# Forgetting attention with a feed-forward layer on one core: the first twelve heads' exponentials go through TensorE transposes instead of an exchange through DRAM

## The chip, the cores and the metric

The kernel runs on one core of one Trainium2 chip. The metric is the device time of the core in microseconds, the median of the runs; smaller is better. Profiled times come from one execution and are counted from the start of its span.

## The reference

Eight batches of eight heads, 576 positions, 64 values per head. All is float32, and the products must come out at nearly that precision.

```python
scores = scale * np.matmul(q, k.transpose(0, 1, 3, 2))
decay = cum[:, :, :, None] - cum[:, :, None, :]      # cum: running sum of log f
scores = np.where(causal, -1e9, scores + decay)
attn = np.exp(scores - scores.max(-1, keepdims=True))
attn = attn / (attn.sum(-1, keepdims=True) + 1e-9)
x = np.matmul(attn, v)          # then tokens x 512
h = x @ w_in                    # 512 -> 2048
out = np.maximum(0.01 * h, h) @ w_out
```

## The kernel before

**Two kinds of work share TensorE.** One is attention, head by head. The other is the feed-forward layer over groups of 256 tokens, 18 of them, cut into pieces that the program calls quanta. A quantum is either half of a pair of hidden blocks (12 matmuls of 256 columns, tile `h`) or half of its product with `w_out` (6 matmuls of 512 columns, tile `o`). `fill(n)` (line 756) takes the next quanta of the generator `ffn` (line 671) and puts them between attention's steps. A float32 product is made of three matmuls on rounded high parts and low parts; that is why each operand is split, `gh` by VectorE and `gl` by GpSimd for the hidden values.

**An early stage** computes the first 256 tokens of three batches, with the order left to the framework's scheduler, which places each instruction where its own estimate finds its engine free. These heads' exponentials are transposed on TensorE (tile `tre`). Thirty-six quanta are placed in this stage.

**The main stage** then goes through 64 heads, here called head 0 to head 63 (`t` in the program). Heads 0 to 39 have all five chunks of query rows, 64 rows in the first and 128 in each of the others; heads 40 to 63 leave out the rows that the early stage has done. From line 810 on (`ordered[0] = True`) every engine keeps the order in which the program issues. That order comes from a table, `PLANS`: each head has eight slots, `scores` of chunk i stands in slot i, and every other step of head `t` stands a given number of slots after the head's first. One head goes so:

- `load` (278) fetches `qraw` and `kraw`; `load_decay` (440) fetches two rows of decays into the operands `s2` and `m2`; `prepare` (448) fills the rest of `s2` and `m2` by two ScalarE copies and two GpSimd subtractions; `split` (460) makes `s1` and `m1` by two ScalarE copies. `s1`, `m1`, `qraw` and `kraw` have one buffer each, `s2` and `m2` two (`a` for even heads, `b` for odd ones, which lets heads be told apart in the trace).
- `scores` (481) has two matmuls for each of six score tiles (`sc`, two buffers in PSUM; the last chunk has two tiles). VectorE subtracts the decay mask and takes the row maximum (out `z`, `max`), ScalarE takes the exponential in place.
- `turn` (530) transposes the exponentials in blocks of 32 by 32 on VectorE, from `z` to `zt`. `send` (555) writes `zt` to DRAM in four DMAs and `receive` (563) reads it back into `pl`, so that the blocks come to lie as the 128 by 128 transposes. This is done in two parts, chunks 0 to 2 and chunks 3 and 4. `divide` (569) rounds `pl` into the high part `ph` on ScalarE and leaves the low part in `pl` on VectorE.
- `values` (577) has 16 matmuls of `ph` and `pl` with the values (tile `av`, which shares two PSUM buffers, tag `tr`, with `rt`); `add` collects two heads in `x`. After each odd head, `inverse`, `spread_inverse` and `fetch_inverse` bring the inverse row sums through DRAM (`rt`, `inv`, `rb`), and `normalise` writes `x` to DRAM (`xd`), where the feed-forward layer fetches it. A batch's tokens are ready for the layer after its eighth head is normalised, 18 slots after that head's first, so in the second head behind it.

How many quanta go into a head is set when it begins: the quanta ready by then, divided by the heads until the batch after is ready and three more, at most nine. All of SyncE's DMAs stand in one queue in the program's order, each behind what the one ahead of it waits for.

Of the kernel before, what the change touches and what calls it, by code (L numbers as in the profile page):

```python
# [8 lines left out]
F32 = mybir.dt.float32  # L9
F32R = mybir.dt.float32r  # L10
# [4 lines left out]
ALU = mybir.AluOpType  # L15
# [61 lines left out]
def forgetting_attention_ffn(ctx, tc, qT, kT, v4, vr, f, w_in, w_out, out):  # L77
# [101 lines left out]
    def minus(out, a, b):  # L179
        nc.gpsimd.tensor_tensor(out, a, b, op=ALU.subtract)  # L180
# [91 lines left out]
    def places(t):  # L272
        return PLANS[0 if t < NEAR else 2 if tasks[t][1] else 1]

# [143 lines left out]
    def fix():  # L418

        for x in "ab":  # L420
            for w, n in (("s2", 2), ("m2", 4)):
                m = S + REST if w == "s2" else S
                y = fixed[w + x] = one.tile([P, m], F32R, tag=w + x, name=f"fixed_{w}{x}")
                nc.gpsimd.memset(y[:D].bitcast(F32), 0.0)
                nc.gpsimd.memset(y[:n].bitcast(F32), 1.0)
                if w == "s2":
                    nc.gpsimd.memset(y[:, :REST].bitcast(F32), 0.0)
            y = fixed["sum" + x] = one.tile([P, 2, NCH], F32, tag="sum" + x, name=f"fixed_sum{x}")
            nc.gpsimd.memset(y, 1.0)
        zt[0] = one.tile([P, 4 * FW], F32, tag="zt", name="zt")  # L430
        nc.gpsimd.memset(zt[0], 0.0)
        for w in ("ph", "pl"):
            fixed[w] = one.tile([P, 4 * FW], F32R, tag=w, name=f"fixed_{w}")
# [4 lines left out]
        nc.gpsimd.memset(vm[:, :, NFULL], 0.0)  # L438

    def load_decay(t):  # L440

# [6 lines left out]
    def prepare(t):  # L448

        s, c0, c1 = tasks[t]  # L450
        h = state[t]
        a, n = c0 * P, width(c1 - 1)
        x = "ab"[t % 2]
        s2, m2 = h["s2"], h["m2"] = fixed["s2" + x][:, REST:], fixed["m2" + x]
        for y, x, lo in ((s2, h["q"], a), (m2, h["k"], 0)):
            nc.scalar.copy(y[D:, lo:n], x[D:, lo:n])
        minus(h["q"][D:, a:n], h["q"][D:, a:n], s2[D:, a:n].bitcast(F32))
        minus(m2[D:, :n], h["k"][D:, :n], m2[D:, :n].bitcast(F32))

    def split(t, which=0):  # L460

# [19 lines left out]
    def scores(t, i):  # L481
# [2 lines left out]
        h = state[t]  # L484
        m, n, at = rows(t, i), width(i), width(i) - P
        part = slice(P - m, P)
        z = h[f"z{i}"] = one.tile([P, n], F32, tag="z" + "ab"[i % 2], name=f"z{i}_{t}")
        z = z[part]
# [16 lines left out]
        if i == NCH - 1 and t + 1 < len(tasks) and places(t)["SIN"]:  # L505
            split(t + 1)
        last = i + len(parts) - 1
        nc.scalar.activation(
# [15 lines left out]
    def unit(t, i, j):  # L524

        if tasks[t][1]:
            return 0, PW, (3 * j if j < 4 else 11) + i - 2 - max(j - 2, 0)
        return *(A if i < B[2] else B)[:2], FULL[i, j]

    def turn(t, i):  # L530
# [21 lines left out]
        base, w, u = unit(t, i, i)  # L552
        nc.vector.transpose(ap(zt[0][part], base + u * Q, [w, 2]), z[:, i * P:i * P + 2 * Q])

    def send(t, part):
# [21 lines left out]
    def values(t, part):  # L577
# [14 lines left out]
        for y, tile_ in enumerate(("ph", "pl")):  # L592
            for j in range(hi):
                i = max(j, lo)
                u = base + unit(t, i, j)[2] * Q
                a = fixed[tile_][:, u:u + 1]
                a = bass.AP(tensor=a.tensor, offset=a.offset, ap=[a.ap[0], [w, 4], [1, (hi - i) * Q]])
# [209 lines left out]
            values_of(x)  # L807
        fill(FQ[x])
    fix()
    beside[0] = ordered[0] = True  # L810
    load(0)
    load_decay(0)
    prepare(0)
    split(0)

    def spread(t, i):

        if tasks[t][1] and not tasks[t - 1][1] and i == 2:
            nc.gpsimd.memset(zt[0][:, :4 * PW], 0.0)
        turn(t, i)  # L820

    def finish(t):
        normalise(t)
# [13 lines left out]
    def load_next(t):  # L837
# [1 line left out]

    N, WT = 8, (1, 1, 1, 1, 1, 1, 1, 1)  # L840
    RANK = [
        split_next, receive, send, load_next, inverse, spread_inverse, divide, values, add, finish, prepare_next,
        load_decay_next, split_v, load_v, fetch_inverse,
    ]
    load(1)
    todo = {}
    for t in range(nt):
        part = int(not tasks[t][1])
        odd = tasks[t][0] % 2
        w = places(t)  # L850
# [22 lines left out]
    for at in range(N * nt + 3 * N):  # L873
# [52 lines left out]
```

## Time and profile before

| | us |
|---|---|
| median of three runs | 1207.67 (1207.54 to 1211.1) |
| the profiled execution's own time | 1206.35 |
| its span, first to last instruction | 1204.6 |
| TensorE busy | 1138.7 |
| VectorE, ScalarE, GpSimd busy | 746.9, 705.7, 445.6 |

Busy time of TensorE includes the overlapping ends of pipelined matmuls. The granted clock is the share of TensorE's full clock, 0.978 on the mean. "Idle before" a group of instructions is time in which its engine had nothing, and the name behind the arrow is what ended it.

### The profile page before, as it was taken

To read this page: it belongs to the slowest core of one execution; us is meant where nothing else is said; L and a number is where in the kernel's file an instruction comes from. 1 tells how busy PE (TensorE), PEld (TensorE's weight loads), DVE (VectorE), ACT (ScalarE), POOL (GpSimd) and SP (SyncE) were. 2 spreads that over 40 slices of the span, in tenths; PEclk is the share of its full clock that TensorE was granted. 3 is DMA by queue.
4 is the path that set the end of the run, shared out by engine and by line. 5 is a ranking of instruction groups with operands and counts; after the bars stand their busy time and mean duration, and the time that the engine had idled before them with its cause. 6 is when DMAs were issued, how large, how long until landed. Compare 5 with 4: busy or idle time off the path is not lost.

```text
span 1204.6 us, 21918 instructions
## 1 busy us (share of the span) xinstructions
PE 1138.7 (95%) x7148; PEld 1010.4 (84%) x7148; DVE 746.9 (62%) x1982; ACT 705.7 (59%) x1555; POOL 445.6 (37%) x353
## 2 busy tenths in 40 slices
PE   9999888879998999999999999999999998989998
PEld 6677777768897998889998899899989997778987
DVE  6878367776675767657676766655567666752221
ACT  7877466766666656666666665555565556541111
POOL 1001434434453445435454444453445454522000
PEclk9999899989998999989999999999999999999999
DMA  6654477876767776776766666656556566651000
GB/s 220 198 181 162 121 220 217 252 220 203 237 203 216 223 230 187 217 223 191 220 199 207 196 217 194 194 167 185 173 179 206 173 193 211 197 175 35 31 18 19
DMA packets 145714, 220.12 MB, mean 183 GB/s; under 512 B 21760, under 2 KB 104560, under 8 KB 145600
## 3 DMA queue, kind: packets, MB, share of 16 engines
q1 hardware_dynamic: 145600, 218.72, 59.7%
q8 instruction: 57, 0.93, 0.3%
q14 instruction: 57, 0.47, 0.1%
HBM read 141.87 MB, written 76.78 MB: 182 GB/s over the span
## 4 chain that ended last, share of the span: by engine, by line
PE 65%; ACT 9%; DVE 9%; DMA 9%; issue 5%; SPq 3%; POOL 1%; ACTq 0%; DVEq 0%; POOLq 0%
PE o L60 25%; PE h L60 24%; PE av L60 6%; PE sc L60 5%; DVE fixed_pl L60 3%; ACT z L60 3%; DMA fixed_pl<-zd 3%; SPq L60 3%; ACT fixed_ph L60 2%; DMA qraw<-in_qT 2%; DVE z L60 2%; PE ave L60 2%; DMA inv<-rt 1%; DMA zd<-zt 1%; PE sce L60 1%
## 5 line engine op out<-in xcount | busy, mean ns | idle before, releaser
L60 PE MATMUL h<-xh,win_h 128*128 128x256 f32 x1152 | 330.5, 287 | 0.4 <-ACT xh L60 0.4
L60 PE MATMUL h<-xh,win_l 128*128 128x256 f32 x1152 | 325.6, 283 | 0.0
L60 PE MATMUL h<-xs,win_h 128*128 128x256 f32 x1024 | 289.1, 282 | 0.0
L60 ACT ACTIVATE z<-z,max 64x64 f32<-64x64 f32 (+3 forms) x272 | 160.5, 590 | 211.8 <-DVE max L60 209.7
L60 POOL TENSOR_TENSOR gl<-g,gh 128x512 fp32r<-128x512 f32 x119 | 154.7, 1300 | 215.4 <-DVE gh L60 191.8
L60 PE MATMUL o<-wout_h,gh 128*128 128x512 f32 x576 | 234.4, 407 | 0.0
L60 PE MATMUL o<-wout_l,gh 128*128 128x512 f32 x576 | 230.0, 399 | 0.0
L60 PE MATMUL o<-wout_h,gl 128*128 128x512 f32 x576 | 229.6, 399 | 0.0
L60 PEld LDWEIGHTS h<-xh,win_h 128*128 128x128 f32 x1152 | 219.9, 191 | 5.7 <-ACT xh L60 0.9
L60 PEld LDWEIGHTS h<-xh,win_l 128*128 128x128 f32 x1152 | 220.0, 191 | 0.1
L60 DVE TENSOR_TENSOR fixed_pl<-fixed_pl,fixed_ph 128x768 fp32r<-128x768 f32 x168 | 158.7, 975 | 98.7 <-ACT fixed_ph L60 98.7
L60 DVE CUSTOM_DVE_ANT_0 z<-sc,tri 64x64 f32<-64x64 f32 (+3 forms) x272 | 123.7, 455 | 133.6 <-PE sc L60 127.1
L60 PEld LDWEIGHTS h<-xs,win_h 128*128 128x128 f32 x1024 | 195.5, 191 | 3.3
L60 DVE STREAM_TRANSPOSE zt<-z 64x64 f32<-64x64 f32 (+4 forms) x528 | 163.2, 346 | 40.8 <-ACT z L60 34.5
L60 ACT ACTIVATE g<-h 128x512 f32<-128x512 f32 x144 | 85.7, 595 | 155.4 <-PE h L60 139.7
L60 DVE CAST gh<-g 128x512 fp32r<-128x512 f32 x144 | 72.2, 501 | 115.4 <-ACT g L60 113.8
L60 ACT CAST fixed_ph<-fixed_pl 128x768 fp32r<-128x768 f32 x168 | 120.6, 755 | 28.5 <-DMA fixed_pl<-zd 27.4
L60 PE MATMUL sc<-m,fixed_s 128*128 128x64 f32 (+2 forms) x336 | 104.4, 316 | 30.0 <-DVE max L60 24.1
L60 PEld LDWEIGHTS o<-wout_h,gl 128*128 128x128 f32 x576 | 109.3, 190 | 26.3 <-POOL gl L60 0.7
L60 PEld LDWEIGHTS o<-wout_h,gh 128*128 128x128 f32 x576 | 109.9, 191 | 18.4 <-issue 0.5
L60 PEld LDWEIGHTS o<-wout_l,gh 128*128 128x128 f32 x576 | 110.0, 191 | 17.6 <-issue 0.3
L60 POOL TENSOR_TENSOR fixed_vs<-fixed_vm,fixed_vs 128x320 fp32r<-128x320 f32 x64 | 70.5, 1101 | 93.1 <-ACT fixed_vs L60 56.1
(116 smaller groups left out, 1669.1 us busy)
## 6 DMA issues: line engine op xcount, KB each, us to landing
zd<-zt SPq DMA_DIRECT2D x160, 144.0 KB
fixed_pl<-zd SPq DMA_DIRECT2D x40, 576.0 KB
kraw<-in_kT SPq DMA_DIRECT2D x128, 144.0 KB
zd<-zt SPq DMA_DIRECT2D x96, 192.0 KB
fixed_pl<-zd SPq DMA_DIRECT2D x24, 768.0 KB
zd<-zt SPq DMA_DIRECT2D x160, 96.0 KB
fixed_pl<-zd SPq DMA_DIRECT2D x40, 384.0 KB
qraw<-in_qT SPq DMA_DIRECT2D x80, 144.0 KB
```

The source lines that it names most:

```text
L60: ins = f(*args, **kw)
```

## The change

For heads 0 to 11 (`FEW = 12`) the exchange is left out. The exponentials are written straight into `zt`, which has room for one head (15 blocks of 128 by 128). `transposes(t, n)` turns them on TensorE in four groups of three or four blocks, each group into one PSUM buffer of the tag `tr` (two buffers, now shared by these groups, `av` and `rt`). ScalarE copies a group from PSUM as the rounded `ph`, VectorE subtracts it from the same PSUM tile into `pl`. The values' matmuls read `ph` and `pl` at other places, with the same number of columns.

For these heads `split_near` takes the place of `prepare` and `split`: it makes `s1` and `m1` by the same two copies, moves half of `s1` into `s2` by a DMA within SBUF in place of one copy, and has GpSimd's two subtractions write `s1` and `m2`. It stands at the end of the head before, not spread over it.

The order of heads 0 to 11 is left to the framework's scheduler; the table of slots begins with head 12. Their quanta are placed by the same rule, in nine eighths of its measure, and a batch is counted as ready at the end of the head after its last one. Head 11's transposes and values stand in head 12's slots, and then `blank` clears on GpSimd the places of `zt` that the exchange leaves unwritten.

```diff
+FEW = 12
...
+    def split_near(t):
...
+        nc.scalar.copy(s1, h["q"])
+        nc.scalar.copy(m1, h["k"])
+        nc.sync.dma_start(s2[D:].bitcast(F32), s1[D:].bitcast(F32))
+        load_decay(t)
+        minus(s1[:D], h["q"][:D], s1[:D].bitcast(F32))
+        minus(m2[D:], h["k"][D:], m1[D:].bitcast(F32))
+        split_v(t)
...
+        if t < FEW:
+            z = h[f"z{i}"] = zt[0][:, i * (i + 1) // 2 * P:(i + 1) * (i + 2) // 2 * P]
...
+    TURNS = (
+        ((0, 0), (1, 1), (1, 0)), ((2, 0), (2, 1), (2, 2), (4, 4)), [(3, j) for j in range(4)],
+        [(4, j) for j in range(4)],
+    )
+    def transposes(t, n):
+        some = TURNS[n]
+        ps = psum.tile([P, 512], F32, tag="tr", name=f"tr_{t}_{n}")[:, :len(some) * P]
+        for x, (i, j) in enumerate(some):
+            nc.tensor.transpose(
+                ps[:, x * P:(x + 1) * P], state[t][f"z{i}"][:, j * P:(j + 1) * P], ident
+            )
...
+        nc.scalar.copy(hi, src)
+        nc.vector.tensor_tensor(lo, src, hi.bitcast(F32), op=ALU.subtract)
...
+    for t in range(FEW):
+        if t:
+            load(t + 1)
+            if (t + 1) % 2 == 0 and t + 1 < FEW:
+                load_v(t + 1)
+        step = rate(t)
+        fill(step)
+        for i in range(NCH):
+            if t and i < len(TURNS):
+                transposes(t - 1, i)
+            scores(t, i)
+            fill(step)
+            if t and i == 1 and tasks[t - 1][0] % 2:
+                inverse(t - 1)
+                spread_inverse(t - 1)
+                fetch_inverse(t - 1)
+        if t:
+            for part in range(2):
+                values(t - 1, part)
+                add(t - 1, part)
+                fill(step)
+            if tasks[t - 1][0] % 2:
+                finish(t - 1)
+        if t + 1 < FEW:
+            split_near(t + 1)
+        else:
+            load_decay(t + 1)
+            prepare(t + 1)
+            split(t + 1)
+            load(t + 2)
+        fill(step * (1 if t else 3))
+    ordered[0] = True
...
+    plan = [(8, transposes, n) for n in range(len(TURNS))] + [(8, clear)]
```

**How the order moves.** The names carry the head as their first number: `sc_6_1_0` is head 6, chunk 1. On TensorE, inside head 6, there stood before, from the second score tile to the next quantum:

```order
L60 MATMUL sc_6_1_0_2510<-m1_6_2408,fixed_s1_1488 128x192
L60 MATMUL sc_6_1_0_2510<-fixed_m2a_1470,fixed_s2a_1466 128x192
L60 MATMUL sc_6_2_0_2521<-m1_6_2408,fixed_s1_1488 128x320
L60 MATMUL sc_6_2_0_2521<-fixed_m2a_1470,fixed_s2a_1466 128x320
L60 MATMUL rt_5_2528<-ident_r_91,r_5_2455 10x128
L60 MATMUL o_2_1_0_2537<-wout_h_0_109,gh_2_0_2353 128x512
```

Between the same two score tiles stand now two groups of head 5's transposes (`tr_5_1` and `tr_5_2`), and a matmul of the feed-forward layer:

```order
L61 MATMUL tr_5_1_2474<-ident_r_91,zt_1484 128x128 x4
L61 MATMUL sc_6_1_0_2481<-m1_6_2428,fixed_s1_1488 128x192
L61 MATMUL sc_6_1_0_2481<-fixed_m2a_1470,fixed_s2a_1466 128x192
L61 MATMUL rt_5_2489<-ident_r_91,r_5_2486 10x128
L61 MATMUL sc_6_2_0_2504<-m1_6_2428,fixed_s1_1488 128x320
L61 MATMUL sc_6_2_0_2504<-fixed_m2a_1470,fixed_s2a_1466 128x320
L61 MATMUL h_2_2_2509<-xh_2_2009,win_h_2_95 128x256
L61 MATMUL tr_5_2_2497<-ident_r_91,zt_1484 128x128 x4
```

So three tiles of the tag `tr` (`tr_5_1`, `rt_5`, `tr_5_2`) now follow each other on TensorE, where one stood. On VectorE, in the same head, there stood before the mask steps (ISA) among the block transposes:

```order
L60 TENSOR_TENSOR fixed_pl_1487<-fixed_pl_1487,fixed_ph_1486 128x768
L60 CAST gh_2_1_2498<-g_2_1_2472 128x512
L60 ISA z1_6_2509,max_6_2475<-sc_6_1_0_2510,tri_144 128x192
L60 ISA max_6_2475 128x1
L60 STREAM_TRANSPOSE zt_1484<-z0_6_2474 64x2x32
L60 TENSOR_TENSOR x_4_2414<-av_4_1_2483,y_4_1_2494 64x4x2x32
L60 ISA z2_6_2520,max_6_2475<-sc_6_2_0_2521,tri_144 128x320
L60 ISA max_6_2475 128x1
L60 STREAM_TRANSPOSE zt_1484<-z1_6_2509 128x4x32
L60 STREAM_TRANSPOSE zt_1484<-z1_6_2509 128x2x32
```

There stand now the mask steps among the subtractions from PSUM:

```order
L61 TENSOR_TENSOR fixed_pl_1487<-tr_5_0_2455,fixed_ph_1486 128x384
L61 TENSOR_TENSOR fixed_pl_1487<-tr_5_1_2474,fixed_ph_1486 128x512
L61 ISA zt_1484,max_6_2461<-sc_6_1_0_2481,tri_144 128x192
L61 ISA max_6_2461 128x1
L61 ISA zt_1484,max_6_2461<-sc_6_2_0_2504,tri_144 128x320
L61 ISA max_6_2461 128x1
L61 TENSOR_TENSOR fixed_pl_1487<-tr_5_2_2497,fixed_ph_1486 128x4x128
L61 ISA zt_1484,max_6_2461<-sc_6_3_0_2529,tri_144 128x448
```

The block transposes are gone, and the score tile of chunk 3 is now read behind the subtraction of `tr_5_2`.

**How the quanta move**, counted from the two orders: heads 0 to 12 hold 70 quanta before (46 in heads 0 to 8, 1 in head 9) and 77 now (48 and 8); heads 13 to 25 hold 95 before and 89 now, heads 26 to 38 hold 108 in both; from head 39 on the two orders differ by one quantum at a time at most, and the last head and what follows it hold 89 before and 90 now. Ahead of head 13's first score tile stand the values' matmuls of 11.4 heads before (182 of 16 each) and of 12 now, and now the 180 transposes of heads 0 to 11.

More of the change, by code (lines that the diff above doesn't have):

```diff
@@ L432, in fix @@
         for w in ("ph", "pl"):
-            fixed[w] = one.tile([P, 4 * FW], F32R, tag=w, name=f"fixed_{w}")
+            fixed[w] = one.tile([P, 16 * P], F32R, tag=w, name=f"fixed_{w}")
         s1 = fixed["s1"] = one.tile([P, S + REST], F32R, tag="s1", name="fixed_s1")
@@ L438, in fix, with blank @@
         nc.gpsimd.memset(vm[:, :, NFULL], 0.0)
+    def blank():
+        for base, w, us in ((A[0], A[1], (0, 3, 5)), (B[0], B[1], (6, 8))):
+            x = zt[0][:, base:base + 4 * w].rearrange("p (b c) -> p b c", b=4)
+            for u in us:
+                nc.gpsimd.memset(x[:, 2:, u * Q:(u + 1) * Q], 0.0)
+                if base + u == 0:
+                    nc.gpsimd.memset(x[:REST, :2, :Q], 0.0)
     def load_decay(t):
@@ L458, in prepare @@
         minus(m2[D:, :n], h["k"][D:, :n], m2[D:, :n].bitcast(F32))
+    def split_near(t):
+        s, c0, c1 = tasks[t]
+        h = state[t]
+        x = "ab"[t % 2]
+        s1 = h["s1"] = fixed["s1"][:, REST:]
+        m1 = h["m1"] = one.tile([P, S], F32R, tag="m1", name=f"m1_{t}", bufs=1)
+        s2, m2 = h["s2"], h["m2"] = fixed["s2" + x][:, REST:], fixed["m2" + x]
+        nc.scalar.copy(s1, h["q"])
[5 more added lines that the diff above has]
+        split_v(t)
     def split(t, which=0):
@@ L486, in scores @@
         part = slice(P - m, P)
-        z = h[f"z{i}"] = one.tile([P, n], F32, tag="z" + "ab"[i % 2], name=f"z{i}_{t}")
-        z = z[part]
+        if t < FEW:
+            z = h[f"z{i}"] = zt[0][:, i * (i + 1) // 2 * P:(i + 1) * (i + 2) // 2 * P]
+        else:
+            z = h[f"z{i}"] = one.tile([P, n], F32, tag="z" + "ab"[i % 2], name=f"z{i}_{t}")
+        z = z[part, :n]
         if i == c0:
@@ L553, in turn @@
         nc.vector.transpose(ap(zt[0][part], base + u * Q, [w, 2]), z[:, i * P:i * P + 2 * Q])
+    NEARBY = {(0, 0): 0, (1, 1): 1, (1, 0): 2, (2, 0): 4, (2, 1): 5, (2, 2): 6, (4, 4): 7}
+    NEARBY.update({(i, j): 5 + i + 2 * j for i in (3, 4) for j in range(4)})
+    TURNS = (
[9 more added lines that the diff above has]
+            )
+        at, step = NEARBY[some[0]], NEARBY[some[1]] - NEARBY[some[0]]
+        hi, lo = (
+            fixed[y].rearrange("p (u c) -> p u c", c=P)[:, at:at + (len(some) - 1) * step + 1:step]
+            for y in ("ph", "pl")
+        )
+        src = ps.rearrange("p (u c) -> p u c", c=P)
+        nc.scalar.copy(hi, src)
+        nc.vector.tensor_tensor(lo, src, hi.bitcast(F32), op=ALU.subtract)
     def send(t, part):
@@ L594, in values @@
                 i = max(j, lo)
-                u = base + unit(t, i, j)[2] * Q
+                if t < FEW:
+                    u = NEARBY[i, j] * P
+                    step = NEARBY[i + 1, j] * P - u if i + 1 < hi else P
+                    dims = [[Q, 4], [step, hi - i], [1, Q]]
+                else:
+                    u = base + unit(t, i, j)[2] * Q
+                    dims = [[w, 4], [1, (hi - i) * Q]]
                 a = fixed[tile_][:, u:u + 1]
-                a = bass.AP(tensor=a.tensor, offset=a.offset, ap=[a.ap[0], [w, 4], [1, (hi - i) * Q]])
+                a = bass.AP(tensor=a.tensor, offset=a.offset, ap=[a.ap[0], *dims])
                 nc.tensor.matmul(
@@ L809, in forgetting_attention_ffn @@
     fix()
-    beside[0] = ordered[0] = True
+    beside[0] = True
     load(0)
-    load_decay(0)
-    prepare(0)
-    split(0)
+    load_v(0)
+    split_near(0)
+    load(1)
     def spread(t, i):
@@ L820, in spread, with clear @@
         turn(t, i)
+    def clear(t):
+        blank()
     def finish(t):
@@ L841, in forgetting_attention_ffn @@
     RANK = [
-        split_next, receive, send, load_next, inverse, spread_inverse, divide, values, add, finish, prepare_next,
+        transposes, clear, split_next, receive, send, load_next, inverse, spread_inverse, divide, values, add, finish, prepare_next,
         load_decay_next, split_v, load_v, fetch_inverse,
     ]
-    load(1)
     todo = {}
-    for t in range(nt):
+    for t in range(FEW, nt):
         part = int(not tasks[t][1])
```

13 lines of the change are left out of this document (11 added, 2 removed).

## The prediction

> **What bounds the kernel now.** I read the page first, for the engine that is nearly always busy, then busy time by stage, then the waits of that engine in the stage that changes, then the timeline at the heads' starts. The page:
>
> ```profile
> span 1204.6 us, 21918 instructions
> PE 1138.7 (95%) x7148; PEld 1010.4 (84%) x7148; DVE 746.9 (62%) x1982; ACT 705.7 (59%) x1555; POOL 445.6 (37%) x353
> PE   9999888879998999999999999999999998989998
> PEclk9999899989998999989999999999999999999999
> ```
>
> TensorE bounds the whole, but its row dips to 8 and 7 in the fifth to ninth slices, and the clock dips there too. By stage (busy time of TensorE, its weight loads, VectorE, ScalarE, GpSimd; then clock, DMA share, GB/s):
>
> ```profile
> 0.00:120.00 120.00, 114.19 (x665) 84.73 (x666) 94.30 (x239) 92.07 (x214) 7.85 (x20) 1.00 0.59 191
> 132.80:254.80 122.00, 106.92 (x638) 93.26 (x639) 81.80 (x250) 80.30 (x184) 49.95 (x38) 0.95 0.73 218
> 254.80:316.60 61.80, 54.55 (x333) 49.32 (x331) 42.94 (x121) 42.27 (x96) 25.55 (x20) 0.92 0.72 223
> 316.60:515.20 198.60, 188.23 (x1230) 171.43 (x1228) 135.11 (x381) 129.61 (x291) 90.33 (x66) 0.97 0.72 213
> ```
>
> The second row is heads 0 to 8, the third heads 9 to 12, the fourth heads 13 to 25. In the first two of these stages no engine is full: TensorE has 88% and a clock of 0.95 and 0.92, VectorE 67% and 69%. So a chain of waits bounds them. TensorE's waits from 128.5 to 316.6 us:
>
> ```profile
> PE sc L60 <- DVE max L60: 11.8, 15, 1.5
> PE av L60 <- ACT fixed_ph L60: 7.9, 6, 2.1
> PE sc L60 <- ACT fixed_s L60: 5.5, 3, 3.6
> ```
>
> Score tiles wait for VectorE's mask step, which stands among the block transposes; value products wait for data that come back from DRAM; and a head waits once for its split operands. The heads' starts, from the timeline of TensorE:
>
> ```profile
> 128.26 0.28 PE L60 MATMUL h<-xh,win_l 128*128 128x256 f32 x1
> 132.14 0.42 PE L60 MATMUL sc<-m,fixed_s 128*128 128x64 f32 x1 [3.61 <-ACT fixed_s L60]
> 316.56 0.19 PE L60 MATMUL sc<-m,fixed_s 128*128 128x64 f32 x1
> 333.32 0.19 PE L60 MATMUL sc<-m,fixed_s 128*128 128x64 f32 x1
> 348.35 0.19 PE L60 MATMUL sc<-m,fixed_s 128*128 128x64 f32 x1
> 515.12 0.30 PE L60 MATMUL sc<-m,fixed_s 128*128 128x64 f32 x1
> ```
>
> These are the last quantum ahead of head 0, then the starts of heads 0, 13, 14, 15 and 26. Head 0 begins after 3.61 us of nothing.
>
> **The unit prices.** How many matmuls of the feed-forward layer lie in heads 0 to 12, in heads 13 to 25, and in head 14, first `h`, then `o`:
>
> ```profile
> 132.80:316.60 183.80, 56.52 (x408) 53.99 (x408) 10.08 (x17) 0.94 0.73 220
> 316.60:515.20 198.60, 76.30 (x576) 72.31 (x576) 14.22 (x24) 0.97 0.72 213
> 333.30:348.30 15.00, 6.27 (x48) 5.85 (x48) 1.19 (x2) 1.00 0.77 230
> ```
>
> ```profile
> 132.80:316.60 183.80, 58.76 (x216) 41.35 (x216) 2.63 (x4) 1.19 (x2) 0.94 0.73 220
> 316.60:515.20 198.60, 73.15 (x283) 50.73 (x282) 0.00 (x0) 3.50 (x6) 0.97 0.72 213
> 333.30:348.30 15.00, 6.12 (x25) 4.36 (x24) 0.00 (x0) 0.00 (x0) 1.00 0.77 230
> ```
>
> At 12 `h` and 6 `o` each these are 70, 95 and 8 quanta. Their pace, and that of a transpose, from the timeline:
>
> ```profile
> 119.91 0.28 PE L60 MATMUL h<-xl,win_h 128*128 128x256 f32 x1
> 120.03 0.28 PE L60 MATMUL h<-xh,win_l 128*128 128x256 f32 x1
> ...
> 121.62 0.55 PE L60 MATMUL tre<-ident_r,zt_early 128*128 128x128 f32 x3
> 121.92 0.48 PE L60 MATMUL o<-wout_l,gh 128*128 128x512 f32 x1
> 122.24 0.39 PE L60 MATMUL o<-wout_h,gl 128*128 128x512 f32 x1
> 122.47 0.40 PE L60 MATMUL o<-wout_h,gh 128*128 128x512 f32 x1
> ```
>
> An `h` follows the next after 0.12 us and an `o` after 0.23: a quantum is 1.41 or 1.38, call it 1.39. Head 14 is full from end to end, 15.03 us with 8 quanta, which leaves 3.9 for its attention; by columns (3200 of scores, 3840 of values) 1.8 and 2.1. Three transposes take 0.30, so 0.10 each.
>
> The Trainium skill, page "TensorE: Matmul & The Clock Gate", section "Part 4: PE-mode transpose", has about 275 ns for a transpose in a kernel. By that the 180 transposes would be 49.5 us, not 18. This trace decides against it: 275 ns is about how long one lasts (0.55 us for three that overlap), and the next matmul starts after 0.30 us for three.
>
> **From 128.5 us to head 13.** Before, 188.1 us (128.5 to 316.6). TensorE's work in it is 70 x 1.39 = 97.3, scores 13 x 1.8 = 23.4, values 11.4 x 2.1 = 23.9: 144.6. So 43.5 us are lost: 25.2 in the three rows of waits, about 11 to the clock (5% of 122 us and 8% of 61.8), the rest in short gaps. After, by the counts of the order: 77 x 1.39 = 107.0, scores 23.4, values 12 x 2.1 = 25.2, transposes 180 x 0.10 = 18.0: 173.6. All 18 lie on the path, since TensorE is what the stage is to be filled with. The 7 quanta more are work that is taken from later heads.
>
> What is still lost, step by step, with these durations:
>
> ```profile
> L60 DVE STREAM_TRANSPOSE zt<-z 64x64 f32<-64x64 f32 (+4 forms) x528 | 163.2, 346 | 40.8 <-ACT z L60 34.5 <-POOL zt L60 3.3
> L60 ACT COPY pte<-tre 128x384 f32<-128x384 f32 x12 | 5.7, 474 | 3.8 <-PE tre L60 3.8
> L60 DVE TENSOR_TENSOR part<-o,part 128x512 f32<-128x512 f32 x4 | 2.6, 678 | 0.0
> L60 ACT COPY part<-o 128x512 f32<-128x512 f32 x4 | 2.3, 589 | 1.1 <-PE o L60 1.1
> L60 POOL TENSOR_TENSOR qraw<-qraw,fixed_s2a 64x576 f32<-64x576 f32 (+1 forms) x32 | 39.2, 1224 | 104.7 <-ACT fixed_s2a L60 94.8 <-PE sc L60 7.3 <-issue 2.6
> L60 POOL TENSOR_TENSOR fixed_m2a<-kraw,fixed_m2a 64x576 fp32r<-64x576 f32 x32 | 46.1, 1440 | 1.6 <-DVE max L60 1.1 <-ACT fixed_m2a L60 0.5
> L60 POOL MEMSET zt<- 128x1920 f32 (+1 forms) x2 | 3.1, 1546 | 4.7 <-ACT g L60 4.6
> L60 ACT CAST m<-kraw 128x576 fp32r<-128x576 f32 x64 | 42.4, 663 | 4.6 <-PE sc L60 4.5
> ```
>
> *The new wait: a group's PSUM buffer.* A group is freed by a copy (0.59 for 512 columns) and then a subtraction (0.68): with hand-overs 1.4 us. The next tile but one of the tag needs that buffer, and behind it on TensorE's queue everything waits. In head 6 the order shows `tr_5_1`, `rt_5`, `tr_5_2`: beside the 1.4 us stand only two score tiles, `rt_5` and one `h`, about 0.7, and results reach PSUM some 0.2 late, so 0.9 is lost; with a late mask step for the last tile, 1.05. In head 5, by the order, six `o` stand between the groups and hide it; there the mask step of chunk 3 comes behind two subtractions (2 x 0.68), and the last tile waits about 0.65. The mean is 0.85, over heads 1 to 11 9.4 us. Head 12 has all four groups in a row, with only the two-step release beside them: 2.0. VectorE has room for this: it loses nine block transposes a head (9 x 0.35 = 3.1 us), and the subtractions stand in place of as many as before.
>
> *The step that is moved: `split_near`.* It stands after a head's last score tile, where before half of it was done ahead. Its chain is a copy (0.66), a second copy or GpSimd's subtraction (1.22), a second subtraction (1.44): about 3.4 us, or the copy and the DMA of half of `s1`, bounded by the landing of a load of like size, from the chain of waits:
>
> ```profile
> 204.31 3.32 DMA qraw<-in_qT
> ```
>
> With the copy that is 4.0 us. Beside it TensorE has, by the order, from 4.5 us (head 0: two quanta of each kind and a group) to 8: covered, and if a quantum were missing, 1 us a head would show. The DMA's place on SyncE's queue is behind `rb`, which waits for `inv`; that is issued some 5 us earlier in the head. Ten DMAs a head leave this queue, so it waits less than before. The 3.61 us ahead of head 0 go, since its splits are hoisted among the early stage's instructions: counted in the 43.5.
>
> *Other.* `blank` is six small memsets, together less than clearing the whole of `zt` (1.5 us, the row of GpSimd above); VectorE's first block transpose of head 12 stands behind that head's second mask step, which waits longer, so I count nothing, and 1.5 once if that cover is gone. Fetched groups are split on VectorE and GpSimd ahead of a head's operands, 1.0; one stretch of clock loss, 1.7. Together 9.4 + 2.0 + 1.0 + 1.7 = 14.1. Bounds for it: 5.3 (0.3 a head and head 12), and 26 (two buffer waits a head).
>
> So head 13 starts at 128.5 + 173.6 + 14.1 = 316.2, 0.4 us earlier, with 7 quanta more done.
>
> **Heads 13 on.** They hold 95 - 6 = 89 quanta. Six fewer are 8.3 us where TensorE is full, as in head 14; head 13, 16.8 us for the same work, was not. I take 0.8 of it: 6.6. From head 26 the orders agree; one quantum more at the end costs 1.4, of which 0.7 was idle time earlier. Sum: -0.4 - 6.6 + 0.7 = -6.3 us. The profiled execution's 1206.35 lies 1.3 below the median of 1207.67, so 1200.1 against its own time and **1201.4** against the median.
>
> **The rivals.**
>
> *Nearly no stalls.* The scheduler's order hides the buffers, as in the early stage, whose 114.2 busy of 120 us, with groups of the same kind, speak for it. Losses 5.3, sum -15.1: 1192.6. Chance 0.10.
>
> *The groups' buffers decide (slower).* Each of 48 groups waits for copy and subtraction on two engines that also serve scores and the hidden layer. The forecast has 0.2 us per group; at 0.45 it is 21.6, with the other 4.7 26.3, and the sum is +5.9: 1213.6. It decides from 0.4. For it: ScalarE and VectorE take score tiles and groups in one order, and a late one holds both. Against it: VectorE is at 67% and becomes freer. Chance 0.15.
>
> *Given back nothing.* Heads 13 to 25 do not get shorter, because the exchange bounds them: heads 0 to 8 took 13.6 us each (122.0 by 9) with 5.1 quanta by the order (11 us of work). Then -0.4 + 0.7: 1208.0. Against it: head 14's full 15 us. Chance 0.12.
>
> *The clock.* After idle time it fell to a half:
>
> ```profile
> 131.40:138.10 6.70, 5.72 (x16) 4.72 (x17) 2.12 (x10) 2.22 (x7) 2.63 (x2) 0.50 0.47 134
> ```
>
> If transposes did not keep it up, three such stretches would cost 3 x 3.4 in place of the 1.7: +2.2, 1209.9. Against it: 1.00 over the first 120 us, with transposes in them. Chance 0.07. The Trainium skill (same page and section) has transposes not counting as busy time for the clock gate; by that rule this rival is the likelier, and the first row by stage does not show it, though transposes are thinner there.
>
> That the change does not do what it says is excluded: the order shows groups and no exchange.
>
> **How the numbers follow.** The forecast's own case has 0.56, between -13 and -3.7. A measurement of this kernel can tell about 0.3% (3.6 us). Faster: 0.56 + 0.10 = 0.66. Same: 0.12 + 0.07 = 0.19. Slower: 0.15. The range reaches from 1191, a little beyond the case of few stalls, to 1211, which leaves out most of the slower one.
>
> **What would show it.** Right: head 13 near 316 us; head 9 full; three transposes 0.30; TensorE's waits for `ph` gone, with waits of `tr` for VectorE's `pl` in their place, 0.2 us a group; heads 13 to 16 each about 1.1 shorter. Wrong: waits of `tr` over 0.4 a group, score tiles waiting for `m2` or `s2`, a clock below 0.95 in heads 1 to 12, or heads 14 and 16 still at 15 us.

## The result, and the profile after

The changed kernel takes **1188.25 us** (1187.84 to 1189.61, four runs) against 1208.22 (1207.54 to 1211.1) for the kernel before on the same chip: a ratio of 0.983, 95% interval 0.981 to 0.985. That is 20 us less, where 6.3 were forecast; the time lies below the range. The profiled execution took 1188.41 us (before: 1206.35), so the profiles differ by 18.0 us of span. From the page after:

```profile
span 1186.6 us, 21867 instructions
PE 1143.6 (96%) x7328; PEld 1018.0 (86%) x7328; DVE 717.5 (60%) x1886; ACT 691.0 (58%) x1543; POOL 445.2 (38%) x359
PE   9999999999998999899999999999999998999998
PEclk9999999999998999999999999999999999999999
```

The dips of the fifth to ninth slices are gone from both rows. What is left of such dips begins in the thirteenth slice, behind the part that was changed. By stage (columns as before: TensorE, weight loads, VectorE, ScalarE, GpSimd; clock, DMA share, GB/s), heads 0 to 8, 9 to 12 and 13 to 25:

```profile
128.80:244.40 115.60, 114.53 (x799) 104.73 (x797) 67.29 (x185) 72.16 (x181) 51.68 (x41) 1.00 0.36 104
244.40:311.00 66.60, 63.38 (x432) 57.09 (x431) 32.84 (x94) 38.00 (x91) 25.68 (x25) 1.00 0.34 97
311.00:500.40 189.40, 179.28 (x1160) 161.81 (x1158) 130.47 (x376) 127.78 (x288) 85.85 (x64) 0.98 0.74 220
```

TensorE is busy for 99% of heads 0 to 8 (88% before) at a clock of 1.00 (0.95 before). The DMA's share there falls from 0.73 to 0.36, since the exchange is gone, and VectorE's load falls too. All that TensorE waited for between 128.5 us and head 13:

```profile
PE h L61 <- POOL xs L61: 1.3, 1, 1.3
PE tr L61 <- DVE fixed_pl L61: 1.1, 1, 1.1
PE rt L61 <- DVE r L61: 0.5, 1, 0.5
PE sc L61 <- DVE max L61: 0.5, 2, 0.3
PE tr L61 <- ACT rt L61: 0.4, 1, 0.4
```

These are 3.8 us, where three rows alone had 25.2. The waits for a group's buffer are the two rows of `tr`: 1.5 us for 48 groups, 0.4 of it in head 4 and 1.1 in head 12. The prediction had 11.4.

Heads 13 and 26 begin now, by the timeline of TensorE, at

```profile
310.98 0.19 PE L61 MATMUL sc<-m,fixed_s 128*128 128x64 f32 x1
499.96 0.19 PE L61 MATMUL sc<-m,fixed_s 128*128 128x64 f32 x1
```

so the third row by stage above ends 0.4 us inside head 26. Where the 18.0 us lie, by the first score tile of a head, with the quanta by the order (a quantum is worth 1.39 us):

| stretch | before, us | after, us | difference | quanta | won for the same quanta |
|---|---|---|---|---|---|
| 128.5 us to head 13 | 188.1 | 182.5 | -5.6 | 70 to 77 | -15.3 |
| heads 13 to 25 | 198.6 | 189.0 | -9.6 | 95 to 89 | -1.3 |
| head 26 to the end | 689.4 | 686.6 | -2.8 | one fewer | -1.4 |

The last column takes 1.39 us off the difference for every quantum more that a stretch holds, and adds as much for every one fewer. So 15 of the 18 us are won in the changed stretch, but only 5.6 are seen there: the rest is work that was done early and need not be done in later heads.

### The profile page after: what moved, and what is told of

The parts are those of the page before. It is cut to its first block, busy times and chain, and to the rows that moved or that the text cites. A ratio compares the mean times of both kernels' runs of the same rounds, so it can differ in the third digit from the quotient of the medians.

```text
span 1186.6 us, 21867 instructions
## 1 busy us (share of the span) xinstructions
PE 1143.6 (96%) x7328; PEld 1018.0 (86%) x7328; DVE 717.5 (60%) x1886; ACT 691.0 (58%) x1543; POOL 445.2 (38%) x359
## 4 chain that ended last, share of the span: by engine, by line
PE 71%; DVE 8%; ACT 7%; DMA 7%; issue 4%; SPq 1%; POOL 1%; ACTq 0%; DVEq 0%; POOLq 0%
PE h L61 27%; PE o L61 26%; PE av L61 7%; PE sc L61 5%; DMA fixed_pl<-zd 3%; DVE fixed_pl L61 3%; PE ave L61 2%; DVE z L61 1%; SPq L61 1%; ACT z L61 1%; PE sce L61 1%; ACT fixed_ph L61 1%; PE warm L61 1%; DMA kraw<-in_kT 1%; DVE zt L61 1%
## 5 line engine op out<-in xcount | busy, mean ns | idle before, releaser
L61 ACT ACTIVATE z<-z,max 128x576 f32<-128x576 f32 (+5 forms) x212 | 126.8, 598 | 159.6 <-DVE max L61 157.1
L61 DVE TENSOR_TENSOR fixed_pl<-fixed_pl,fixed_ph 128x768 fp32r<-128x768 f32 x132 | 123.4, 966 | 72.9 <-ACT fixed_ph L61 72.8
L61 DVE CUSTOM_DVE_ANT_0 z<-sc,tri 128x288 f32<-128x288 f32 (+5 forms) x212 | 98.0, 462 | 105.6 <-PE sc L61 101.3
L61 DVE CAST gh<-g 128x512 fp32r<-128x512 f32 x144 | 77.7, 540 | 123.0 <-ACT g L61 121.7
L61 DVE STREAM_TRANSPOSE zt<-z 64x256 f32<-64x256 f32 (+6 forms) x420 | 129.9, 347 | 29.6 <-ACT z L61 24.1
L61 ACT CAST fixed_ph<-fixed_pl 128x768 fp32r<-128x768 f32 x132 | 95.7, 763 | 22.0 <-DMA fixed_pl<-zd 21.3
L61 POOL TENSOR_TENSOR fixed_vs<-fixed_vm,fixed_vs 128x320 fp32r<-128x320 f32 x64 | 66.6, 1041 | 79.2 <-ACT fixed_vs L61 62.9
```

Source lines behind the costliest of these rows:

```text
L61: ins = f(*args, **kw)
```

## The experiments

The theory with which they began: what is won is idle time and half clock that the exchange's chain leaves in the early heads; a transpose costs the 0.1 us of its place in the stream; and the groups' buffers cost little because the scheduler's order puts other work behind them. Three runs test the price, the buffers and the order, and one the rival that the order alone makes the gain. All ratios are to the kernel before on the same chip.

**Each transpose issued twice** (180 more, into the same places):

```diff
+            for _ in range(2):
                 nc.tensor.transpose(
```

> Every transpose of heads 0 to 11 is issued twice into the same place (360 instead of 180). Theory A (TensorE is full in these heads, and a transpose costs its pace, 0.109 us): 180 x 0.109 = +19.6 us on the changed kernel's 1188.3, so about 1207, and the cores' span grows by as much between heads 1 and 12. Rival B (transposes fill time in which TensorE would wait anyway): less than +5, so under 1193. Rival C (a transpose costs its duration of 0.27): +49, so about 1237.

Measured: 1208.6 us, ratio 1.0015 (0.9996 to 1.0034). Head 13 starts at 327.1 us, 16.1 later, so 0.089 for each added transpose. The stretch from head 0 to head 13:

```profile
128.40:327.10 198.70, 196.31 (x1408) 181.88 (x1406) 100.58 (x279) 112.68 (x271) 77.71 (x66) 1.00 0.32 91
```

TensorE is full and its clock is 1.00 with 360 transposes among 1408 recorded matmuls. A transpose therefore costs its place in the stream, on the path, and nothing hides it. The whole kernel became 20 us longer; the 4 to 5 us beyond these 16.1 lie behind head 13, where the edit changes nothing, and no run explains them.

**Each group's subtraction issued twice**, so that its buffer comes free some 0.69 us later, 33 us in all:

```diff
+        for _ in range(2):
             nc.vector.tensor_tensor(lo, src, hi.bitcast(F32), op=ALU.subtract)
```

> VectorE's subtraction of each group is issued twice, so that a group's PSUM buffer is freed 0.69 us later (48 x 0.69 = 33 us more of VectorE). Theory A (the buffers are freed well ahead of need, and VectorE has room): +1 to +5 us, 1189 to 1193. Rival D, the step of the prediction that had each head lose 0.85 us to these buffers: TensorE waits for most of the added time, +20 to +33, 1208 to 1221.

Measured: 1193.4 us, ratio 0.9886 (0.986 to 0.9911), 5 to 7 us above the change. TensorE's waits for buffers:

```profile
PE tr L61 <- DVE fixed_pl L61: 6.0, 8, 1.8
```

Of 33 us of added release time some 5 become waits: eight waits for 48 groups. With the subtraction issued once, the change has one such wait. Head 13 starts 7.7 us later (318.7). That is a little more than the theory had and far from the 20 of its rival, and it is what makes the prediction's rival "the groups' buffers decide" fall.

**The program's order from head 4 on**, in place of the scheduler's:

```diff
     for t in range(FEW):
+        if t == 4:
+            ordered[0] = True
```

> From head 4 on every engine keeps the program's own order; the transposes stay. Theory A (the gain is the exchange's absence): within 3 us of 1188.3. Rival E (the scheduler's order is what fills TensorE): heads 4 to 11 lose about what they lost before, 1 to 2 us a head, 1196 to 1204.

Measured: 1229.1 us, ratio 1.0183 (1.0166 to 1.02): 41 us above the change and slower than before. TensorE's waits from 128.5 to 320 us, of which the first six:

```profile
PE sc L61 <- DVE max L61: 10.1, 7, 2.4
PE rt L61 <- DVE r L61: 4.9, 4, 2.0
PE sc L61 <- DMA fixed_m2b<-dec_k: 4.5, 3, 1.5
PE sc L61 <- POOL fixed_s L61: 3.1, 3, 1.4
PE sc L61 <- POOL fixed_m2a L61: 3.1, 3, 1.2
PE h L61 <- DVE xh L61: 2.1, 1, 2.1
```

The third to fifth rows are the chain of `split_near`. On ScalarE the two casts that begin it stand in the program's order behind five other instructions that they have no need of (from the order, head 6 with head 7's casts):

```
L61 ACTIVATE zt_1484,fixed_sumb_1482<-zt_1484,max_6_2461 128x448
L61 ACTIVATE zt_1484,fixed_sumb_1482<-zt_1484,max_6_2461 128x576
L61 ACTIVATE g_2_2_2555<-h_2_2_2509 128x512
L61 COPY y_5_0_2564<-av_5_0_2557 64x384
L61 COPY y_5_1_2578<-av_5_1_2567 64x256
L61 CAST fixed_s1_1488<-qraw_7_2438 128x576
L61 CAST m1_7_2593<-kraw_7_2441 128x576
```

and in the changed kernel the scheduler has hoisted them behind the exponential of chunk 3:

```
L61 ACTIVATE zt_1484,fixed_sumb_1482<-zt_1484,max_6_2461 128x448
L61 CAST fixed_s1_1488<-qraw_7_2438 128x576
L61 CAST m1_7_2593<-kraw_7_2441 128x576
L61 ACTIVATE zt_1484,fixed_sumb_1482<-zt_1484,max_6_2461 128x576
```

So the order is a condition of the gain. The theory had it at a few us and was wrong by tens; its rival, that the scheduler's order is what fills TensorE, had the direction, but its 1196 to 1204 was 25 us too low.

**The same, with the splits put early by hand** (`load_decay` at the head's start, `split_near` behind the last score tile, ahead of the values):

```diff
+        if t >= 4 and t + 1 < FEW:
+            split_near(t + 1)
...
-            split_near(t + 1)
```

> Program order from head 4 on, as in the run before it that lost 41 us, but with two things written earlier: the next head's decays are loaded at the head's start, ahead of the DMA that waits for s1, and split_near stands right behind the last score tile, ahead of the values' copies. Theory F (program order lost its time because the next head's operands came late: ScalarE's two copies stood behind five other instructions, and the decays' loads behind the DMA of s1): most of it comes back, 1190 to 1203. Rival E (the rest of the scheduler's order is what counts): 1215 or more.

Measured: 1215.4 us, ratio 1.0063 (1.0044 to 1.0081). That is the rival's outcome (1215 or more). The waits for GpSimd's operands and for decays are gone but for 0.4 us, and a third of the 41 us with them. The rest goes with VectorE's order, though no run changes that order alone. VectorE's subtractions in this kernel, from 180 to 331 us, and in the changed one, from 179 to 311 (count, busy us, mean ns, idle before):

```profile
L61 DVE TENSOR_TENSOR fixed_pl<-tr,fixed_ph 128x512 fp32r<-128x512 f32 (+1 forms) x36 | 23.6, 658 | 47.1 <-ACT fixed_ph L61 47.1
```

```profile
L61 DVE TENSOR_TENSOR fixed_pl<-tr,fixed_ph 128x512 fp32r<-128x512 f32 (+1 forms) x36 | 23.1, 655 | 10.3 <-ACT fixed_ph L61 9.6
```

In the program's order a group's subtraction stands ahead of the next mask step, so VectorE waits 47.1 us for ScalarE's copies while score tiles lie ready behind it; the scheduler puts the mask steps ahead of them, and 10.3 us are left. TensorE waits 10.6 us for mask steps here, and 0.5 in the changed kernel.

**No transposes, but the scheduler's order for heads 0 to 11**, with the exchange:

```diff
-    beside[0] = ordered[0] = True
+    beside[0] = True
...
+        if at == 12 * N:
+            ordered[0] = True
```

> The kernel before, with the exchange through DRAM, but heads 0 to 11 in the order of the framework's scheduler. Theory A (the exchange's chain loses the time, in whatever order): 1202 to 1211. Rival E (the order does it): 1188 to 1196.

Measured: 1253.0 us, ratio 1.0377 (1.0347 to 1.0408), beyond what either theory expected; the run could not test either. The scheduler drew quanta forward, so that heads 6 to 9 and 11 hold none, and TensorE waits for the splits. The first two rows of its waits from 128.5 to 320 us:

```profile
PE sc L60 <- ACT m L60: 20.7, 7, 4.9
PE av L60 <- ACT fixed_ph L60: 9.3, 10, 2.9
```

So the free order with the exchange was no gain. What it is worth by itself cannot be told, since the quanta moved with it.

**Head 9 filled in the kernel before, and starved in the changed one.** Before, head 9 holds one quantum and takes 12.8 us; now it holds eight. In the first edit (on the kernel before) it gets eight, in the second (on the changed kernel) the measure of 1.2 that it had before:

```diff
+        if t == 9:
+            step = 1.0
```

```diff
-        step = rate(t)
+        step = 1.2 / N if t == 9 else rate(t)
```

> The kernel before, but head 9 is given one quantum a slot (8 in all) from the 13 that are left, where it had 1. Theory A (heads 9 and 10 lose 12 us to idle time and clock, and the quanta can fill some of it; the exchange's waits stay): 3 to 7 us faster than before, ratio 0.994 to 0.9975. Rival G (the changed kernel gains by where its quanta lie, not by the transposes): 12 us or more faster, ratio under 0.990.

> The changed kernel, but head 9 is given the kernel before's measure (1.2 quanta a head in place of 8). Theory A: TensorE idles in head 9 for some 4 us, some of them at half clock after it, and the quanta lie in full heads later: +3 to +8 us, ratio to before 0.986 to 0.990. Rival G: +12 or more, ratio 0.993 or more.

Measured: 1205.4 us, ratio 0.9979 (0.995 to 1.0008), and 1190.9, ratio 0.9858 (0.9828 to 0.9889). Head 9's quanta are worth 2 to 3 us in either direction, near what can be told from nothing: the gain is not theirs.

**Other numbers of heads.** `FEW` is the only edit in each:

```diff
-FEW = 12
+FEW = 20
```

> Transposes for heads 0 to 19 in place of 0 to 11. Before, heads 12 to 19 lost little but for head 17 (about 9 us, starved of quanta, after the batch's end). Theory A (a head's transposes cost 1.5 us and pay where the exchange's waits and starved heads lose more): 8 x 1.5 = 12 us more work against 9 to 14 regained, so within 4 us of the changed kernel, ratio 0.980 to 0.987. Rival H (each head with transposes gains as heads 0 to 11 did, 1.5 us): 12 us faster than it, ratio 0.974 or less.

> The change with FEW = 16. Theory A (heads 13 to 15 are full before and hold no idle time; transposes cost there 1.5 us a head that comes back only as far as those heads hide something else): 1189 to 1195, between twelve heads (1188) and twenty (1194). Rival J (each head with transposes gains the same 1.7 us): 1181 to 1183. The run with twenty heads speaks for A; this one tells whether twelve is near the best.

> The change with FEW = 8. Theory A (the gain is idle time in the heads that hold too few quanta; before, heads 0 to 8 lose some 27 of the 43.5 us and heads 9 to 12 some 16): about half to two thirds of the gain, 1193 to 1201 against a before of 1208; TensorE waits stay in heads 9 to 12. Rival I (the start alone): 1188 to 1191, the same as with twelve. Rival J (each head with transposes gains the same, 20/12 = 1.7 us): 1194 to 1196, and sixteen heads would be at 1181 to 1183.

> The change with FEW = 4: four heads with transposes, the exchange from head 4 on. Theory A (the gain is the idle time that the exchange's chain leaves in the heads that hold too few quanta to cover it; each such head that gets transposes gives back its own share): before, heads 0 to 3 are the first 48 us of the 188, so about a quarter to a third of the 43.5 us lost lies there, less 4 x 1.5 us of transposes; between 2 and 9 us faster than before, 1199 to 1206 against a before of 1208, and heads 5 to 12 still show the waits of score tiles for VectorE and of values for fixed_ph. Rival I (the gain belongs to the start alone: the 3.6 us ahead of head 0 and the first heads without a predecessor): nearly all of the 20 us, 1188 to 1193.

| heads with transposes | median, us | ratio (95%) |
|---|---|---|
| 4 | 1190.9 | 0.9874 (0.9844 to 0.9904) |
| 8 | 1189.5 | 0.9848 (0.9817 to 0.988) |
| 12 | 1188.25 | 0.9832 (0.9814 to 0.985) |
| 16 | 1194.2 | 0.9894 (0.9867 to 0.9921) |
| 20 | 1194.3 | 0.9889 (0.9856 to 0.9922) |

Beyond twelve, transposes cost more than they give: with sixteen as the theory had it, with twenty 2 us more than its 4. With twenty, heads 13 to 25 take 195.3 us instead of the changed kernel's 189.0: 120 transposes more are 10.7 us at 0.089 and one quantum more is 1.4, so only 5.8 of these 12.1 are won back there. With sixteen they take 190.9, and what follows 693.0 instead of 686.6, although it holds two quanta fewer. Why is open; the trace shows that values wait longer for `ph`, first with sixteen heads (from 310 us on), then with twelve:

```profile
PE av L61 <- ACT fixed_ph L61: 20.8, 12, 4.8
```

```profile
PE av L61 <- ACT fixed_ph L61: 9.8, 7, 3.4
```

Below twelve the theory failed: four heads give some 15 of the 20 us, where it expected 2 to 9, and eight nearly all. Both times are those of its rival, that the gain belongs to the start alone; the run after this one tests that cause. The stretches of the run with four heads (0 to 3, 4 to 12, 13 to 25, and from 26):

```profile
128.80:179.30 50.50, 49.43 (x335) 44.80 (x334) 27.83 (x78) 31.60 (x77) 24.04 (x19) 1.00 0.37 104
179.30:308.60 129.30, 113.96 (x697) 101.06 (x695) 87.84 (x263) 87.50 (x199) 52.02 (x46) 0.93 0.74 213
308.60:500.90 192.30, 187.15 (x1231) 171.13 (x1229) 134.33 (x378) 129.87 (x291) 88.25 (x65) 0.98 0.73 218
500.90:1187.30 686.40, 663.45 (x4236) 601.76 (x4236) 390.29 (x988) 355.00 (x761) 265.10 (x203) 0.99 0.55 166
```

In the changed heads the theory holds: heads 0 to 3 are full, and heads 4 to 12 still lose 15 us of idle time and 7% of the clock. Head 13 starts 8.0 us earlier than before, with as many quanta done (70). The other 9 us come from heads that the edit does not touch: heads 13 to 25 hold 95 quanta in both and take 192.3 us against 198.6, the rest 686.4 against 689.4. In the later profile of the same four-head kernel heads 13 to 25 take 194.3, so some 2 of these us are scatter between executions. TensorE's waits there are 5.1 and 6.5 us, and 10.1 before.

**The start of head 0 alone**, in the kernel before: the order is fixed behind head 0's splits, which may then be hoisted into the early stage.

```diff
-    beside[0] = ordered[0] = True
+    beside[0] = True
     load(0)
     load_decay(0)
     prepare(0)
     split(0)
+    ordered[0] = True
```

> The kernel before, with one thing of the change: the order is fixed behind head 0's four operand steps instead of ahead of them, so that the scheduler may hoist these among the early stage's instructions; the exchange stays for all heads, and from head 0's first score tile on the order and the quanta are those of before. Theory K (four heads with transposes gave almost all of the gain because of the start: the 3.6 us of idle time ahead of head 0 and the half clock of 6.8 us that follows it): 3.6 and 3.4 us go, 1200 to 1203 against a before of 1208, and the idle time and half clock of heads 2 to 4 stay. Rival L (the whole gain of about 17 is this start, because later stalls depend on it): 1188 to 1193. Rival M (the time is absorbed by the next wait of the exchange, in head 2 or 3): 1206 to 1209, then the gain of the first four heads is that of their transposes.

Measured: 1203.9 us, ratio 0.9968 (0.9951 to 0.9984), between the first and the third theory. In its profile head 0 starts at 128.5 instead of 132.1, head 4 at 184.7 instead of 191.9, head 13 at 310.2 instead of 316.6, and then:

```profile
310.20:509.10 198.90, 189.26 (x1231) 172.50 (x1229) 137.45 (x381) 129.84 (x291) 89.51 (x66) 0.97 0.72 213
509.10:1200.90 691.80, 666.54 (x4236) 604.63 (x4236) 389.14 (x988) 354.67 (x761) 264.84 (x203) 0.99 0.55 164
```

So the start is worth 6.4 us at head 13 and about 4 of the 20 in the end, and heads 13 to 25 do not get shorter by it. It is part of the change: of the 15.3 us won ahead of head 13, some 6 are the start's and some 9 are left for the transposes, if the two simply add. Of the 8.0 us by which head 13 starts earlier with four heads, the start alone gives 6.4.

**What a later head with few quanta shows.** Head 17 holds two quanta in all of these runs, and there the exchange shows. Before, in head 17, ScalarE, VectorE and TensorE:

```profile
383.65 0.83 ACT L60 CAST fixed_ph<-fixed_pl 128x768 fp32r<-128x768 f32 x1 [4.37 <-DMA fixed_pl<-zd]
```

```profile
384.51 0.96 DVE L60 TENSOR_TENSOR fixed_pl<-fixed_pl,fixed_ph 128x768 fp32r<-128x768 f32 x1 [5.76 <-ACT fixed_ph L60]
```

```profile
385.92 0.74 PE L60 MATMUL sc<-m,fixed_s 128*128 128x448 f32 x1 [4.83 <-DVE max L60]
```

Read as one: ScalarE waits 4.37 us for data from DRAM, VectorE behind it 5.76, the mask steps stand behind VectorE's subtraction, and TensorE is idle for 4.83. The page's name for this wait is `max`; its cause is the DMA. From the last 2 us of this idle time on, TensorE's clock was a half:

```profile
383.90:394.10 10.20, 7.34 (x28) 6.38 (x29) 8.12 (x24) 8.04 (x18) 2.92 (x3) 0.50 0.55 156
```

In the changed kernel the same cast waits 2.54 us:

```profile
371.38 0.83 ACT L61 CAST fixed_ph<-fixed_pl 128x768 fp32r<-128x768 f32 x1 [2.54 <-DMA fixed_pl<-zd]
```

```profile
373.65 0.47 PE L61 MATMUL sc<-m,fixed_s 128*128 128x448 f32 x1 [3.26 <-DVE max L61]
```

```profile
375.00:381.80 6.80, 5.72 (x19) 4.80 (x19) 5.79 (x18) 6.50 (x14) 4.23 (x4) 0.50 0.58 168
```

and with four heads it does not wait at all, in both profiles of that kernel. How long the data keep a starved head waiting thus differs by over 4 us between runs of the same table of slots. But this does not decide the length of the later heads by itself. With the start alone, and the exchange in every head, the same cast waits 1.02 us, and TensorE behind it 2.08; head 17 is shorter, and heads 13 to 25 together are not (198.8 us by the starts of heads 13 and 26, 198.6 before):

```profile
373.55 0.83 ACT L60 CAST fixed_ph<-fixed_pl 128x768 fp32r<-128x768 f32 x1 [1.02 <-DMA fixed_pl<-zd]
```

And a second execution of the changed kernel itself, from the last comparison below, has 1.42 where the first had 2.54:

```profile
369.86 0.83 ACT L61 CAST fixed_ph<-fixed_pl 128x768 fp32r<-128x768 f32 x1 [1.42 <-DMA fixed_pl<-zd]
```

The next two runs take this wait's effect away by filling the starved heads, 17, 25 and 33 in the changed kernel, and 9, 17 and 25 with four heads:

```diff
+        if t in (17, 25, 33) and i == 0:
+            step = 0.75
```

> The changed kernel with six quanta each in heads 17, 25 and 33 (2, 3 and 3 there now), taken from the heads behind them. Theory N (the quanta that the change brings forward are partly given back as idle time and half clock at heads with too few quanta: head 17 of the changed kernel has 5 us of idle time and 6.8 us at half clock): head 17 is full, clock 1.00 there, 4 to 9 us less, 1179 to 1184 against 1188. Rival O (the exchange's chain bounds these heads whatever stands beside it, and later heads miss the quanta): 1187 to 1192.

> Four heads with transposes, and six quanta each in heads 9, 17 and 25. Theory N: the idle time at heads 9 and 17 goes (before it is 5 us and 6.8 us of half clock at head 9 with four heads), 1180 to 1186 against the 1190.9 of four heads; if it comes out below or equal to the twelve heads with filled heads, the transposes of heads 4 to 11 are worth nothing by themselves. Rival O: 1189 to 1194.

Measured: 1183.8 us, ratio 0.9817 (0.9793 to 0.9842), and 1186.6, ratio 0.9837 (0.9814 to 0.986). The changed kernel's heads 13 to 25, when filled:

```profile
311.10:499.80 188.70, 183.25 (x1209) 166.54 (x1207) 133.25 (x381) 131.44 (x294) 89.97 (x65) 1.00 0.74 224
```

TensorE is busy for 183.25 us of 188.70 at a clock of 1.00, against 179.28 of 189.40 at 0.98: five quanta more (94) in the same time. This profile does not show where the 4.4 us between the medians come from, though. Its execution took 1188.37 us, the slowest of the five and as long as the change's, and the heads behind took 686.7 us with five quanta fewer, against 686.6; there the rival came true, that those heads miss the quanta. With four heads, filling gives about as much by the medians, and a kernel with eight heads fewer on transposes comes within 3 us.

**Side by side on one chip**: the change, four heads, and the change with the three heads filled.

> The changed kernel itself, on one chip with the next two, so that differences of 2 to 5 us between them can be read. If twelve heads are better than four by what the single runs showed: 1187 to 1190, ratio 0.982 to 0.985.

> Four heads with transposes, beside twelve on the same chip. Theory P (heads 4 to 11 give back in heads 13 to 25 what they win: their transposes are worth under 2 us): within 2 us of the twelve heads. Rival Q (they are worth the 7 us that the quanta brought forward suggest): 5 to 8 us above the twelve heads.

> The changed kernel with six quanta each in heads 17, 25 and 33, beside the changed kernel on the same chip. Theory N (idle time and half clock at starved heads can be had back by quanta from the heads behind): 3 to 6 us below the changed kernel. Rival O (the heads behind then lack them): within 1.5 us of it.

| | median of six runs, us | ratio (95%) |
|---|---|---|
| twelve heads | 1189.0 (1183.4 to 1189.8) | 0.9841 (0.9811 to 0.987) |
| four heads | 1192.5 (1191.4 to 1193.7) | 0.9877 (0.9854 to 0.9901) |
| twelve heads, three starved heads filled | 1184.5 (1181.2 to 1188.1) | 0.9811 (0.9782 to 0.9839) |

Four heads are 3.4 us above twelve, between the two theories: heads 4 to 11 are worth 0.4 us each. The filled kernel is 4.5 below the change by medians, as it was in the run ahead of this (1183.8); the two intervals overlap, so it is the likely best version, by about 0.3%, not a certain one.

## Why the prediction was right in sign and wrong in size

**What bounds the early heads: right.** No engine was full and a chain of waits bounded them; with the chain gone TensorE fills. From head 0 to head 13 its busy time went from 161.47 us in 183.8 to 177.91 in 182.2.

**The price of a transpose: right.** 0.10 was taken and 0.089 measured by doubling. The prediction weighed against it a figure of the Trainium skill, page "TensorE: Matmul & The Clock Gate", section "Part 4: PE-mode transpose", about 275 ns. The trace has that figure as the duration of one, and it is not what one costs:

```profile
L61 PE MATMUL tr<-ident_r,zt x180: 270/272/330, 138.9 to 298.1; 128*128 128x128 f32 x180
```

**The step that failed: "The next tile but one of the tag needs that buffer ... so 0.9 is lost".** On it rest 9.4 us for heads 1 to 11 and 2.0 for head 12, 0.2 us a group; 0.4 and 1.1 were measured, 0.03 a group. The prediction let the two PSUM buffers go round in turn and had `tr_5_2` wait for the subtraction of `tr_5_1`. The timeline of head 6 after, for ScalarE, VectorE and TensorE:

```profile
208.73 0.25 ACT L61 COPY rt<-rt 10x128 f32<-10x128 f32 x1
```

```profile
208.86 0.69 DVE L61 TENSOR_TENSOR fixed_pl<-tr,fixed_ph 128x512 fp32r<-128x512 f32 x1 [1.61 <-ACT fixed_ph L61]
```

```profile
207.61 0.60 PE L61 MATMUL tr<-ident_r,zt 128*128 128x128 f32 x4
...
208.65 0.28 PE L61 MATMUL h<-xh,win_h 128*128 128x256 f32 x1
209.03 0.66 PE L61 MATMUL tr<-ident_r,zt 128*128 128x128 f32 x4
```

The second group starts at 209.03 us, right behind ScalarE's short copy of `rt` (208.98), while VectorE still reads the first group (until 209.55). So it stands in the buffer that came free first, `rt`'s, not in the one next in turn, and TensorE shows no wait in this head. The other part of the term was a mask step that comes late, 0.65 us in a head such as head 5: TensorE's waits for `max` are 0.5 us in all 13 heads. Where no `rt` stands between, other work covers the release, as the run with two subtractions shows (eight waits for 48 groups, with 0.69 us more each). That the release was read off the allocation order, and not off who frees a buffer when, is the largest error in the stage.

**A second error hid part of it.** The forecast had 14.1 us lost and 8.9 were (182.5 less 173.6), but the waits that the trace names are only 3.8. The other 5.1 went on work that the prediction had priced at 173.6. Before the change its own sum had some 7 us of this kind, "the rest in short gaps" (43.5 less 25.2 and 11); after the change it put them at nothing, without a reason. The two errors work against each other, so that the stage came out only 5.2 us below the forecast is in part luck. Of the 11.7 us between the forecast's 6.3 and the profiles' 18.0, 5.2 lie ahead of head 13, 3.0 in heads 13 to 25 and 3.5 behind.

**The clock: wrong by its whole term.** 1.7 us were set aside and none was lost: the clock is 1.00 over heads 0 to 12, and with twice the transposes too. The rival built on that loss is out. The Trainium skill (same page and section) has transposes not counting as busy for the clock gate; at 180 or 360 of them among other matmuls no run here shows it.

**`split_near` covered: right, on a condition the prediction did not name.** No wait for its operands shows in the changed kernel. The prediction counted the cover from the order and did not say what makes it: in the program's order the same step costs 11 us in waits (the third to fifth rows of its run), and those waits go when its copies are put early by hand.

**Heads 13 to 25: -9.6 us for -6.6.** The prediction took 0.8 of six quanta's 8.3 us, because head 13 had not been full. In full they leave 1.3, and a third less half clock (6.8 us at head 17, 10.2 before) would be 1.7. But the run with four heads got -6.3 there with no quantum fewer (-4.3 in its second profile), so quanta alone do not settle the stretch, and that the prediction came near it is in part luck. The wait in head 17 does not settle it either, as the run with the start alone shows.

**Head 26 to the end: -2.8 for +0.7.** The quanta were miscounted: the end holds one more, but heads 39, 59 and 62 hold one less and head 60 one more, so the stretch holds one fewer, -1.4 instead of +0.7. The prediction's own counts say so: seven more ahead of head 13 and six fewer up to head 26 leave one fewer behind. The other 1.4 us lie within what this stretch scatters between runs of nearly the same order (686 to 692 us in the profiles quoted).

**The rivals.** "Nearly no stalls" was the nearest. In the stage the result lies between it (5.3 us lost) and the forecast; in sum it lies beyond it, because this rival kept the forecast's later heads. "Given back nothing" is out, since the later heads are shorter. What no rival had: half of the gain of four heads falls in heads that were not changed. What remains open is why: the traces show fewer waits there, and data that no longer keep head 17 waiting, not what sets either.

## What to carry to other kernels

Price a change that takes work off a chain by the idle time and the half clock of the stage that it frees, and then follow the freed work into the later stages: here 15 us were won ahead of head 13, some 6 of them by an earlier start, and 10 of the 15 appeared in later heads. A wait for a pool's buffer is read from who frees which buffer when, and a step is covered only in the order in which it is really issued; the same code in the program's order was slower than the kernel before. Where a stage is starved, a few quanta moved into it were worth about as much, by the medians, as eight more heads of the change (4.5 against 3.4 us). A wait in one head should be seen in two executions of a kernel before it is called a cause.

## What the runs showed of the hardware

- An fp32 transpose of 128 by 128 lasts 272 ns and costs 89 ns in a stream of matmuls; 180 more made the stretch 16.1 us longer.
- In these traces the half clock comes with idle time, not with transposes: 10.2 us of it began within an idle time of 4.83, 6.8 us behind one of 3.26, and none came where the same head was filled (clock 1.00), nor with 360 transposes in the stretch ahead of head 13.
- The same transfer, the second part of the exchange read in head 17, kept its reader waiting 4.37 us in one program, 1.02 in another and not at all in a third, with two quanta in the head each time, and 2.54 and 1.42 in two executions of one program.
